# Loading x in larger pieces without a wait, and a new order of all tasks, in a fused attention and gMLP kernel

## Chip, cores and metric

The kernel runs on one core of one Trainium2 chip. The metric is the device time of one execution in microseconds (us), the median of several runs. The core has five engines with a queue each: PE (matrix multiply), DVE (vector), ACT (scalar and activation functions), POOL and SP. Loads and stores are issued by SP, a few by ACT, and are carried out by 16 DMA engines.

## What is computed

Inputs and weights are bf16. x has 2048 tokens of 448 features.

```
h  = x + A(layernorm(x))
h2 = h + B(layernorm(h))

A: qkv = x @ wqkv                       # 16 heads of 28
   each token attends to itself and the 7 tokens 2, 4, ... 14 before it (masked at the start)
   o = softmax(q k^T / sqrt(28)) v;  return o @ wo
B: z = gelu(x @ w_in)                   # 448 -> 2 x 896
   z1, z2 = halves of z;  z2 = layernorm(z2)
   g = w_sp @ z2 + b_sp                 # over the tokens, w_sp is 2048 x 2048
   return (z1 * g) @ w_out
```

## The kernel before

Attention works on nine tiles (`NT`), each of 114 tokens and a halo of 16 before them, in both halves of the sequence at once (s = 0 and 1, 1024 tokens apart), with even and odd tokens on different partitions (w = 0 and 1). A tile of x lies in `xs[:, i, s, :]`. `ln_unit` normalises it: on DVE statistics (`bn1_i_s`, lines 656 and 657) and the normalisation into a ring of four buffers (`nrm1_i_s`, line 674), and in between the reciprocal root (`rs1_i`, two instructions on POOL or ACT). The result is transposed into `xh`: tiles 0 to 2 on PE (`tT1_i`, line 689) with an eviction (`ev1_i`, line 626 or 628), tiles 3 to 8 by a DMA that SP issues (`tD1_i`, line 680) and that stands in SP's queue until the normalisation is done. Matmuls of q and k (`mmq`, `mmk`, line 768) go by groups of tiles: 0; 1; 2 to 4; 5 to 8. They use padded copies of the weights (`cpq`, `cpk`, line 626 on ACT or 628 on DVE); every copy needs all four parts of its weight. Then follow, by tile, v (`mmv`, line 802), scores (`mml`, line 835), exp, the band mask (`mask`, line 857), sums (`mmr`, line 868), the product with v (`mmo`, line 891) and the product with 1/sum (`ot`, line 909).

Then, by blocks of 128 tokens, comes the output projection (`mmy`, line 948) with the residual (`h`, line 956, on x loaded a second time as `x_tm` by the loads `xn0` to `xn3`, line 528), layernorm, a DMA transpose (`tD2`), z2 (`mmz2`, line 968) and z1 (`mmz1`, line 1015), and at the end the product with w_sp (`g`, line 1052, whose result DVE adds the bias to, line 1061) and with w_out (line 1081).

The order is not that of the program text. Every piece of work is a task, numbered as it is created. `SEQ` lists, for SP, POOL, DVE, ACT and PE in this order, the numbers of that engine's tasks in the order of its queue. `Planner.replay` walks through these lists with estimated durations; by them it gives out PSUM banks and ring buffers and emits the instructions. An engine works strictly in its list's order; waits come from the data itself (`Sched.issue`), and a DMA may also wait for tasks in its `waits`. So one late task holds all that stands behind it on its engine.

Before, the x loads of tiles 2 to 8 wait on SP for the q weights:

```
for t in t_xs[i]:
    t.deps += t_w["q"]
    t.waits += t_w["q"]
```

The start of the queues before, with the numbers read as names (`xs2_1` is tile 2, w = 1, both halves of the sequence; `xs0a`, `xs0b` are the halves of tile 0; `wq0` to `wq3` are the parts of the q weight, two of 336 KB and two small ones; `wkv2`, `wkv3` serve k and v; `wo`, `wop` are parts of the output weight):

```
SP   xs1_0 xs0a_1 xs0a_0 xs0b_1 xs0b_0 wq1 wq3 wk0 wop1 wkv3 | xs2_1 xs3_0 xs3_1 xs4_0 xs6_1 xs4_1
     xs2_0 xs7_0 wv0 wv1 xs8_0 xs5_1 wop2 xs8_1 xs6_0 xs5_0 wo1 wop0 tD1_3 xs7_1 tD1_4 wo2 xn1 xn2 ...
ACT  xs1_1 wkv2 wq0 wq2 rs1_1 wk1 rs1_0 ev1_1 cpq1 ev1_0 ...
DVE  bn1_1_0 bn1_1_1 bn1_0_0 nrm1_1_0 nrm1_1_1 bn1_0_1 nrm1_0_0 nrm1_0_1 cpq0 cpk0 cpk1 bn1_3_1 ...
PE   f0 tT1_1 f1 tT1_0 mmq1_0 mmq1_2 mmk1_0 mmk0_0 mmq0_2 mmk1_2 mmq0_0 mmk0_2 mmv0 tT1_2 mml0 mmv1 mmv2 mmk2_1 ...
```

(`f0` and `f1` are 15 and 3 matmuls that only warm PE up; the bar marks where SP waits for the q weights.) The loads of w_sp (`wsp0_b`, `wsp1_b`, line 930) are DMA transposes in two chains of 16, in the order of blocks 0, 8, 1, 9, 2, 10, 3, 11, 4, ...; each waits on SP until the one before it in its chain has landed.

Of the kernel before, what the change touches and what calls it, by code (L numbers as in the profile page):

```python
# [6 lines left out]
D = 448  # L7
DH = 28
FH = 896
# [4 lines left out]
ST = 1024  # L14
# [205 lines left out]
class Planner:  # L220
# [68 lines left out]
    def replay(self, t0=0.7):  # L289
# [13 lines left out]
        for _ in tasks:  # L303
# [34 lines left out]
            if t.nbytes:  # L338
                dma_free = max(dma_free, now + 0.3) + t.nbytes / t.bw / 1000.0
                t.end = dma_free + t.setup  # L340
                self.landed = max(self.landed, t.end)
            else:
                t.end = now + dur + extra
# [11 lines left out]
def bass_sequential_preLN__sliding_local_dilated__mixer_gmlp__prompt_kernel(  # L355
# [18 lines left out]
    with contextlib.ExitStack() as top:  # L374
# [102 lines left out]
        stg_old = r_wl["q"] + [r for i in range(NT) for s in range(2) for r in r_xs[i][s]]  # L477
# [25 lines left out]
        def dve4x(n):  # L503
            return (190.0 + 0.26 * n) / 1000.0

        def dma(eng, name, fn, nbytes, deps=(), reads=(), writes=(), rel=(), store=False, issue=0.5, bw=245.0, after=(), setup=2.0):
            def em():
                rd = list(reads)
                for w in t.waits:
# [645 lines left out]
```

## Time and profile before

| | |
|---|---|
| median of 3 runs | 255.0 us (253.35 to 256.37) |
| the profiled execution, its own time | 255.13 us |
| its span, first to last instruction | 253.4 us |
| PE busy | 237.7 us, 94% of the span |
| DVE, ACT, POOL busy | 138.3, 86.7, 23.4 us |
| mean granted clock of PE | 0.987 |

Busy shares are averages over stages that differ: the first 20 us wait for loads, then attention keeps PE, DVE and ACT busy together, and from about 130 us on PE works almost alone. In a row of the time line, what stands in brackets is how long the engine was idle before it and what ended that. "issue" there means that the profile saw nothing that was waited for.

### The profile page before, as it was taken

What the parts mean: (1) busy time and instruction counts of PE and PEld (TensorE: products, weight loads), DVE (VectorE), ACT (ScalarE), POOL (GpSimd) and SP (SyncE); (2) the same over time, 40 slices, a digit from 0 to 9 for tenths busy, and PEclk for the clock granted to TensorE, in tenths of its full rate; (3) what the DMA queues carried; (4) which work ended last, traced back from release to release, by engine and by line L of the source; (5) the groups of instructions that cost most, each with busy time, mean ns of one, the idle gap of its engine ahead of it and who ended that gap; (6) DMA issues with size and microseconds to landing.
All of it is one profiled execution on the core that took longest, in us unless ns stands there. A gap on an engine that the chain in (4) does not pass through costs nothing.

```text
span 253.4 us, 6573 instructions
## 1 busy us (share of the span) xinstructions
PE 237.7 (94%) x2942; PEld 119.5 (47%) x2952; DVE 138.3 (55%) x278; ACT 86.7 (34%) x110; POOL 23.4 (9%) x61
## 2 busy tenths in 40 slices
PE   7674999987999899999999999999999999999995
PEld 2372665544455454454444444444444444444443
DVE  3585975569599898769881005105700238321573
ACT  2543968676597834857571000000000000000000
POOL 7010200000030203203450000000000000000000
PEclk9997999999799999999999999999999999999999
DMA  5879987568863997695733363310000000010213
GB/s 153 238 189 203 259 97 184 81 106 117 171 169 54 209 221 180 120 131 119 160 84 85 83 153 79 77 26 0 3 0 0 18 0 21 0 36 0 75 36 110
DMA packets 60657, 25.62 MB, mean 101 GB/s; under 512 B 48084, under 2 KB 60484, under 8 KB 60628
## 3 DMA queue, kind: packets, MB, share of 16 engines
q1 hardware_dynamic: 59524, 24.22, 46.1%
q10 hardware_dynamic: 1104, 0.98, 1.4%
q8 instruction: 23, 0.38, 0.6%
q14 instruction: 6, 0.05, 0.1%
HBM read 11.75 MB, written 1.84 MB: 54 GB/s over the span
## 4 chain that ended last, share of the span: by engine, by line
PE 87%; DMA 5%; SPq 4%; issue 3%; DVE 0%
PE psum L1052 38%; PE psum L1081 8%; PE psum L1015 8%; PE psum L768 8%; PE psum L968 7%; PE psum L802 6%; PE psum L948 5%; PE psum L835 3%; SPq L540 3%; PE psum L891 2%; DMA z2p<-in_A_wqkv_dram 2%; DMA xh<-tring 2%; DMA w_in<-in_A_wqkv_dram 1%; PE psum L868 1%; SPq L546 1%
## 5 line engine op out<-in xcount | busy, mean ns | idle before, releaser
L1061 DVE TENSOR_TENSOR ub<-psum,reg 128x512 bf16<-128x512 f32 x28 | 18.8, 687 | 58.5 <-PE psum L1052 40.3
L1052 PE MATMUL psum<-reg,z2p 128*128 128x512 bf16 x219 | 49.2, 379 | 0.3
L1052 PE MATMUL psum<-wspT_lo,z2p 128*128 128x512 bf16 x219 | 48.7, 379 | 0.4 <-issue 0.2
L1052 PEld LDWEIGHTS psum<-wspT_lo,z2p 128*128 128x128 bf16 x224 | 21.8, 98 | 26.5 <-DVE z2p L998 0.4
L1052 PEld LDWEIGHTS psum<-reg,z2p 128*128 128x128 bf16 x224 | 21.8, 98 | 26.5 <-DVE ub L1061 0.4
L768 PE MATMUL psum<-xh,reg 64*128 64x114 bf16 (+3 forms) x448 | 27.2, 271 | 1.1 <-DVE reg L628 1.0
L968 PE MATMUL psum<-w_in,xh 64*128 64x448 bf16 x224 | 22.6, 349 | 0.4 <-DMA xh<-tring 0.4
L1081 PE MATMUL psum<-reg 128*128 128x448 bf16 (+1 forms) x119 | 22.3, 342 | 0.0
L1015 PE MATMUL psum<-xh,w_in 64*128 64x512 bf16 x196 | 22.0, 376 | 0.0
L626 ACT ACTIVATE reg<-psum 128x896 bf16<-128x896 f32 (+4 forms) x24 | 17.8, 758 | 11.0 <-PE psum L802 5.5
L1091 DVE TENSOR_TENSOR tring<-psum,x_tm 128x448 bf16<-128x448 f32 (+1 forms) x17 | 9.8, 594 | 21.1 <-PE psum L1081 21.1
L768 PEld LDWEIGHTS psum<-xh,reg 64*128 64x128 bf16 x448 | 16.3, 93 | 9.9 <-DVE reg L628 1.2
L802 PE MATMUL psum<-w_in,xh 64*128 64x448 bf16 x126 | 15.8, 398 | 4.3 <-issue 4.2
L984 DVE BATCH_NORM_STATS2 st<-z2p 128x6 f32<-128x448 bf16 x32 | 17.5, 611 | 3.2 <-ACT z2p L978 3.2
L850 ACT ACTIVATE reg<-psum 128x928 bf16<-128x928 f32 x18 | 16.4, 943 | 5.4 <-PE psum L835 5.2
L978 ACT ACTIVATE z2p<-psum 128x896 bf16<-128x896 f32 x16 | 13.9, 917 | 9.9 <-PE psum L968 6.5
L1025 ACT ACTIVATE reg<-psum 128x1024 bf16<-128x1024 f32 x14 | 13.9, 1029 | 7.9 <-PE psum L1015 7.9
L1081 PEld LDWEIGHTS psum<-reg 128*128 128x128 bf16 x119 | 11.5, 98 | 10.3 <-DVE tring L1091 0.4
L968 PEld LDWEIGHTS psum<-w_in,xh 64*128 64x128 bf16 x224 | 10.6, 94 | 11.2 <-DMA xh<-tring 0.8
L1015 PEld LDWEIGHTS psum<-xh,w_in 64*128 64x128 bf16 x196 | 9.5, 94 | 11.4
L631 POOL TENSOR_SCALAR rs<-mv 128x2 f32<-128x2 f32 x18 | 5.1, 284 | 105.0 <-DVE mv L657 86.0
L656 DVE BATCH_NORM_STATS2 st<-z2p 128x6 f32<-128x448 bf16 x18 | 11.0, 612 | 6.9 <-DMA z2p<-in_A_x_dram 6.8
(54 smaller groups left out, 202.8 us busy)
## 6 DMA issues: line engine op xcount, KB each, us to landing
w_in<-in_B_w_in_dram SPq DMA_DIRECT2D x4, 672.0 KB, 5.5
x_tm<-in_A_x_dram SPq DMA_DIRECT2D x4, 448.0 KB, 5.2
z2p<-in_A_x_dram SPq DMA_DIRECT2D x15, 112.0 KB, 3.3
out_dram<-tring SPq DMA_DIRECT2D x15, 112.0 KB, 1.8
w_in<-in_A_wqkv_dram SPq DMA_DIRECT2D x3, 336.0 KB, 5.8
reg<-in_A_wo_dram SPq DMA_DIRECT2D x4, 196.0 KB
reg<-in_B_w_out_dram SPq DMA_DIRECT2D x1, 784.0 KB, 5.6
reg<-in_B_b_sp_dram SPq DMA_DIRECT2D x1, 512.0 KB, 4.8
```

The source lines that it names most:

```text
L626: iss("act", lambda e: e.activation(dst, src, AF.Copy), reads=rd, writes=wr)
L768: iss("pe", lambda e, c=c, s=s, gi=gi, lhs=lhs, mov=mov: e.matmul(psum[:, bk[s] * 512 + cw * gi:bk[s] * 512 + cw * gi + cw], lhs, mov, sta ...
L802: iss("pe", lambda e, c=c, s=s: e.matmul(psum[:, bk[s] * 512:bk[s] * 512 + D], xh[64 * s:64 * s + 64, BLK[s][c], 128 * i:128 * i + 128], w ...
L850: iss("act", lambda e: e.activation(E[:, es[0], 2 * n:2 * n + 2, :], pair_view(lb, 0, 8 * JW), AF.Exp, scale=SCALE), reads=[r_bank[lb[0]], ...
L968: iss("pe", lambda e, c=c, s=s: e.matmul(psum[:, zb[s] * 512:zb[s] * 512 + D], xh[64 * s:64 * s + 64, BLK[s][c], 128 * u:128 * u + 128], w ...
L978: iss("act", lambda e: e.activation(z2p[:, u:u + 9:8, D * k:D * k + D], pair_view(zb, 0, D), AF.Gelu_apprx_tanh), reads=[r_bank[zb[0]], r_ ...
L984: iss("dve", lambda e, b=b: e.bn_stats(st3[:, b, k, :], z2p[:, b, D * k:D * k + D]), reads=[r_z2[b][k]], writes=[r_st3[b][k]])
L1015: iss("pe", lambda e, c=c, s=s: e.matmul(psum[:, bk[s] * 512:bk[s] * 512 + 512], w_in[0][64 * s:64 * s + 64, c, 128 * f:128 * f + 128], xh ...
L1025: iss("act", lambda e: e.activation(z1p[f].rearrange("p (s t) -> p s t", s=2)[:, :, 512 * ch:512 * ch + 512], pair_view(bk, 0, 512), AF.Ge ...
L1052: iss("pe", lambda e, b=b: e.matmul(psum[:, gb[0] * 512:gb[0] * 512 + 512], z2p[:, b, 128 * f:128 * f + 128], src[:, b, 512 * (tc % 2):512 ...
L1061: iss("dve", lambda e: e.tensor_tensor(ub[:, us_[0], :], psum[:, gb[0] * 512:gb[0] * 512 + 512], bb[:, 512 * tc:512 * tc + 512], ALU.add), ...
L1081: iss("pe", lambda e, f=f: e.matmul(psum[:, wb[0] * 512 + d0:wb[0] * 512 + d1], z1p[f][:, 128 * m:128 * m + 128], w_out[:, f, d0:d1], star ...
```

## The change

Tiles 3 to 8 of x come in loads of three tiles each, for one half of the sequence and one w (`xs3_10` is tiles 3 to 5, second half, w = 0): eight loads in place of twelve. The wait of x loads for the q weights is dropped. `replay` gets other constants for DMAs (issue 0.62 us and 285 bytes per ns, and 0.4 us ahead of the data), and the dependencies of the statistics are told to it by half of the sequence. All five lists of `SEQ` are new. The constants act only through the lists and the banks and buffers that `replay` hands out; no instruction but the x loads is added or taken away, though some small ones (evictions, copies, the reciprocal roots) move between ACT, DVE and POOL.

```diff
-        for i in range(2, NT):
-            ld_xs(i, 0, "sp")
-            ld_xs(i, 1, "sp")
-            for t in t_xs[i]:
-                t.deps += t_w["q"]
-                t.waits += t_w["q"]
+        ld_xs(2, 0, "sp")
+        ld_xs(2, 1, "sp")
+        for i in (3, 6):
+            for n in range(2):
+                for w in range(2):
+                    ld_xs3(i, n, w, "sp")
...
+        def ld_xs3(i, n, w, eng):
+            lo = ST * n + TQ * i - HALO + w
+            src = X[lo:lo + 2 * TQ + 127, :]
+            src = bass.AP(tensor=src.tensor, offset=src.offset, ap=[[2 * D, 64], [TQ * D, 3], [1, D]])
+            xs_dma("xs%d_%d%d" % (i, n, w), eng, xs[64 * w:64 * w + 64, i:i + 3, n, :], src, 192, [(i + k, n, w) for k in range(3)])
...
-                dma_free = max(dma_free, now + 0.3) + t.nbytes / t.bw / 1000.0
+                dma_free = max(dma_free, now + 0.4) + t.nbytes / t.bw / 1000.0
...
-                tb.append(add("bn%d_%d_%d" % (which, u, n), "dve", 0.76, em, deps=src_deps))
+                tb.append(add("bn%d_%d_%d" % (which, u, n), "dve", 0.77, em, deps=src_deps[n]))
...
-            tt = add("tT%d_%d" % (which, u), "pe", 0.9 if u < 2 else 0.5, em_t, deps=tn + [c_ident], acq=[("ps", 1, bk)],
+            tt = add("tT%d_%d" % (which, u), "pe", 0.55, em_t, deps=tn + [c_ident], acq=[("ps", 1, bk)],
```

The start of the new lists, with names for the numbers:

```
SP   xs1_0 xs0b_1 xs0b_0 xs0a_0 xs0a_1 xs3_10 wk0 wkv3 xs3_11 xs3_00 xs3_01 wq1 wq3 wop2 wop0 wop3 xs2_1 xs2_0 wv1 wv0
     xs6_11 xs6_10 xs6_00 wo0 tD1_3 xs6_01 tD1_4 wo2 xn1 win1_1 wo3 tD1_5 tD1_8 tD1_6 tD1_7 wop1
     wsp0_0 wsp0_8 win1_0 wsp0_1 xn0 wo1 wsp0_9 wsp0_2 xn3 wsp0_10 win1_3 wsp0_3 win1_2 wsp0_11 wsp0_4 xn2 tD2_1 ...
ACT  xs1_1 wkv2 wk1 rs1_1 wq0 rs1_0 wq2 cpk0 ev1_0 evk1_0 evk0_2 cpq0 evq0_2 evk0_0 rs1_2 ...
DVE  bn1_1_1 bn1_0_1 bn1_1_0 bn1_0_0 nrm1_1_0 nrm1_1_1 nrm1_0_0 nrm1_0_1 cpk1 ev1_1 bn1_4_1 bn1_3_1 bn1_4_0 bn1_3_0 cpq1
     nrm1_3_0 bn1_2_0 bn1_2_1 evq1_0 nrm1_3_1 nrm1_2_0 nrm1_2_1 nrm1_4_0 nrm1_4_1 bn1_6_1 bn1_5_0 bn1_5_1 bn1_7_1 bn1_8_1 ...
PE   f0 tT1_1 f1 tT1_0 mmk1_0 mmk0_2 mmk1_2 mmk0_0 mmq0_2 mmq1_0 mmq0_0 mmq1_2 mmv1 tT1_2 mmv0 mmv2 mml0 mmq2_2 mmk2_1 ...
     ... mmk3_3 mmy1 mmo3_0 mmr4 mmo3_1 mmo4_0 mmo4_1 mml5_0 mmv5 ... mmy4 mml8_1 mmr7 mmy5 mmo7 mmr8 mmo8 mmz2_1 ...
```

Later, `tD2_1` comes first of the second transposes instead of `tD2_2`, and the bias load `bb` stands one w_sp load further back than before.

More of the change, by code (lines that the diff above doesn't have):

```diff
@@ L476, in bass_sequential_preLN__sliding_local_dilated__mixer_gmlp__prompt_kernel @@
         kv_old = r_wl["k"] + r_wl["v"]
-        stg_old = r_wl["q"] + [r for i in range(NT) for s in range(2) for r in r_xs[i][s]]
+        stg_old = r_wl["q"] + [r for i in range(NT) for rr in r_xs[i] for r in rr]
         reg2_old = [r for rr in r_q + r_k for r in rr] + [r_qend]
@@ L504, in dve4x, with dma @@
             return (190.0 + 0.26 * n) / 1000.0
-        def dma(eng, name, fn, nbytes, deps=(), reads=(), writes=(), rel=(), store=False, issue=0.5, bw=245.0, after=(), setup=2.0):
+        def dma(eng, name, fn, nbytes, deps=(), reads=(), writes=(), rel=(), store=False, issue=0.62, bw=285.0, after=(), setup=2.0):
             def em():
@@ L532, in ld_x, with xs_dma @@
                 t_x[b] = t
-        t_xs = [[] for _ in range(NT)]
+        t_xs = [[[], []] for _ in range(NT)]
         XT = X.rearrange("(s t) f -> t s f", s=2)
+        def xs_dma(name, eng, dst, src, kb, cover):
+            t = dma(eng, name, lambda e: e.dma_start(dst, src), kb * D * 2, writes=[r_xs[i][n][w] for i, n, w in cover])
+            for i, n, w in cover:
+                t_xs[i][n].append(t)
         def ld_xs(i, w, eng):
@@ L539, in ld_xs @@
             if i:
-                t_xs[i].append(dma(eng, "xs%d_%d" % (i, w), lambda e: e.dma_start(
-                    xs[64 * w:64 * w + 64, i, :, :], XT[lo:lo + 127:2, :, :]), 128 * D * 2,
-                    writes=[r_xs[i][0][w], r_xs[i][1][w]]))
+                xs_dma("xs%d_%d" % (i, w), eng, xs[64 * w:64 * w + 64, i, :, :], XT[lo:lo + 127:2, :, :], 128, [(i, n, w) for n in range(2)])
                 return
-            t_xs[0].append(dma(eng, "xs0a_%d" % w, lambda e: e.dma_start(
-                xs[64 * w + HALO // 2:64 * w + 64, 0, 0, :], X[w:w + 111:2, :]), 56 * D * 2, writes=[r_xs[0][0][w]]))
-            t_xs[0].append(dma(eng, "xs0b_%d" % w, lambda e: e.dma_start(
-                xs[64 * w:64 * w + 64, 0, 1, :], X[ST + lo:ST + lo + 127:2, :]), 64 * D * 2, writes=[r_xs[0][1][w]]))
+            xs_dma("xs0a_%d" % w, eng, xs[64 * w + HALO // 2:64 * w + 64, 0, 0, :], X[w:w + 111:2, :], 56, [(0, 0, w)])
+            xs_dma("xs0b_%d" % w, eng, xs[64 * w:64 * w + 64, 0, 1, :], X[ST + lo:ST + lo + 127:2, :], 64, [(0, 1, w)])
+        def ld_xs3(i, n, w, eng):
[3 more added lines that the diff above has]
+            xs_dma("xs%d_%d%d" % (i, n, w), eng, xs[64 * w:64 * w + 64, i:i + 3, n, :], src, 192, [(i + k, n, w) for k in range(3)])
         t_w = {}
@@ L559, in ld_w @@
             t = dma(eng, "w%s%d" % (p, n), lambda e: e.dma_start(dst, src),
-                    (64 if n > 1 else 384) * len(p) * D * 2, writes=[r_wl[x][n] for x in p], bw=200.0 if n > 1 else 330.0)
+                    (64 if n > 1 else 384) * len(p) * D * 2, writes=[r_wl[x][n] for x in p], bw=285.0)
             for x in p:
@@ L568, in ld_win @@
                 t = dma("sp", "win%d_%d" % (z, n), lambda e, dst=dst, src=src: e.dma_start(dst, src),
-                        (64 if n > 1 else 384) * FH * 2, deps=deps, writes=[r_win[z][n]], bw=200.0 if n > 1 else 330.0, after=after)
+                        (64 if n > 1 else 384) * FH * 2, deps=deps, writes=[r_win[z][n]], bw=285.0, after=after)
                 t_win.setdefault(z, []).append(t)
@@ L704, in bass_sequential_preLN__sliding_local_dilated__mixer_gmlp__prompt_kernel @@
         for i in range(NT):
-            t_xh.append(ln_unit(i, 1, t_xs[i] + ([c_x0] if i == 0 else [])))
+            t_xh.append(ln_unit(i, 1, [t_xs[i][0] + ([c_x0] if i == 0 else []), t_xs[i][1]]))
         fill("f0", 15)
@@ L959, in bass_sequential_preLN__sliding_local_dilated__mixer_gmlp__prompt_kernel @@
             t_h.append(th)
-            t_hT.append(ln_unit(u, 2, [th]))
+            t_hT.append(ln_unit(u, 2, [[th], [th]]))
             tb3 = []
```

58 rows, old and new, of the table SEQ are left out of this document.

## The prediction

> **What bounds the kernel now.** I read the page first, then a table of stages (busy time, granted clock and DMA share in stretches I chose), then the early waits and the time line. The page:
>
> ```profile
> span 253.4 us, 6573 instructions
> PE   7674999987999899999999999999999999999995
> w_in<-in_A_wqkv_dram SPq DMA_DIRECT2D x3, 336.0 KB, 5.8
> x_tm<-in_A_x_dram SPq DMA_DIRECT2D x4, 448.0 KB, 5.2
> ```
>
> TensorE (PE) is nearly full from slice 5 on. Its holes are in the first four slices of 6.3 us; the clock is in the table by stage that follows (columns: stretch, its length, busy us and count of PE, PEld, DVE, ACT, POOL, granted clock, DMA share, GB/s):
>
> ```profile
> 0.00:6.80 6.80, 5.27 (x15) 1.83 (x15) 2.63 (x7) 1.78 (x3) 4.46 (x20) 1.00 0.61 158
> 6.80:9.60 2.80, 1.21 (x10) 0.60 (x10) 2.04 (x7) 1.01 (x3) 0.00 (x0) 1.00 0.90 268
> 12.40:15.60 3.20, 2.34 (x84) 2.22 (x84) 2.56 (x6) 1.20 (x3) 0.23 (x2) 1.00 0.60 147
> 15.60:18.10 2.50, 2.47 (x88) 2.24 (x84) 1.79 (x5) 1.43 (x3) 0.89 (x2) 1.00 0.73 186
> 18.10:22.20 4.10, 0.00 (x0) 0.00 (x0) 3.11 (x10) 2.38 (x7) 0.00 (x0) 1.00 0.89 250
> 22.20:25.80 3.60, 3.54 (x25) 1.78 (x26) 1.78 (x5) 0.78 (x1) 0.19 (x1) 0.53 1.11 191
> ```
>
> From 18.1 to 22.2 PE does nothing, and for the 3.6 us after it runs at 0.53 of its clock. The chain calls the hole "issue", but the loads of the last weights (line 559, issued from 15 to 18 us) say who waits for them:
>
> ```profile
> L559 SPq DMA_DIRECT2D w_in<-in_A_wqkv_dram x2: 489/542/596, 15.6 to 16.3; - x2
>   PE psum L802: 4.2, 1
> DMA to landing us min/median/max: 3.6/4.7/5.9
> ```
>
> The two V loads issue at 15.6 and 16.3; the later one lands at 16.3 + 5.9 = 22.2, where PE starts again. They are late because SP stands still before them:
>
> ```profile
> SPq L176 <- DMA z2p<-in_A_wqkv_dram: 2.4, 1, 2.4
> 6.56 0.47 SPq L559 DMA_DIRECT2D w_in<-in_A_wqkv_dram  x1
> 9.60 5.99 SPq L540 DMA_DIRECT2D z2p<-in_A_x_dram  x8
> ```
>
> SP is idle from 7.0 to 9.6, held by the q weights, then issues eight x loads at about 0.61 us (one takes 1.40) ahead of V. From 12.4 to 18.1 the DMA share is only 0.60 and 0.73: SP's issue sets the rate there, not the memory.
>
> **The change, part by part.** The time line of the front (start, us, engine, line, operation) and the chain after it:
>
> ```profile
> 6.12 0.63 DVE L656 BATCH_NORM_STATS2 st<-z2p 128x6 f32<-128x448 bf16 x1 [0.43 <-DMA z2p<-in_A_x_dram]
> 6.88 0.67 DVE L674 TENSOR_SCALAR tring<-z2p,mv,rs 128x448 bf16<-128x448 bf16 x2
> 7.61 0.56 PE L689 MATMUL psum<-ident,tring 128*128 128x128 bf16 x7 [0.83 <-DVE tring L674]
> 8.01 0.81 PE L620 MATMUL psum<-wspT_lo 128*128 128x512 bf16 x3
> 9.79 1.50 ACT L626 ACTIVATE reg<-z2p 128x1568 bf16<-128x1568 bf16 x1
> 10.42 1.82 PE L768 MATMUL psum<-xh,reg 64*128 64x114 bf16 x56
> 13.26 4.83 PE L768 MATMUL psum<-xh,reg 64*128 64x114 bf16 x168 [1.02 <-DVE reg L628]
> 22.26 2.73 PE psum L802 x14
> 26.47 2.75 PE psum L802 x28
> 29.23 3.10 PE psum L768 x42
> 40.43 1.54 PE psum L768 x14
> ```
>
> *Front of SP.* The first five loads are of the same kinds, so they end near 4.3 as now. Then come xs3_10, wk0, wkv3, three more 168 KB x loads, wq1, wq3, three small wop, two xs2, wv1, wv0. At 0.6 us each (0.4 for a wop) with 0.05 between, wv0 issues at 12.6: 3.7 us earlier, with no wait. With 3.6 to 5.9 us to landing, V is there from 16.2 to 18.5. By bytes: 3.86 MB go before the last V load is done; 1.07 MB have gone by 6.8 (158 GB/s), the rest at 259 (mean of the rows at 268 and 250) takes 10.8 us: 17.6. I take **18**; the upper end, if the DMA can do no more than its 186 GB/s row, is 6.8 + 15.0 = 21.8.
>
> *First matmuls, later.* DVE's list now has bn1_1_1, bn1_0_1, bn1_1_0, bn1_0_0. The second needs tile 0's load, 6.12 by the row above; three statistics at 0.78 end at 8.46, two normalisations at 9.15, so tile 1's transpose moves from 7.61 to 9.2. ACT has wq0's issue (0.55) between the two rstd, so tile 0 is normalised at 10.05; with warm-up matmuls (0.81) the second transpose ends at 11.1. ACT's copy of k (1.50, after wq2's issue at 9.8) ends at 11.3. PE starts k at **11.3 instead of 10.42**. The 224 matmuls take 1.82 + 4.83 = 6.65: 17.95. The copies of q stand behind four statistics of tiles 3 and 4 on DVE (11.2 + 3.1 + 0.62 = 15.0 against 14.6 needed): +0.4. PE now idles 6.8 to 9.2, which may halve its clock for one stretch; between 0 and 2 us, of which I take 0.6. Then q and k end at 19.0 (18.3 to 20.5). V has landed: **V starts at 19.0 instead of 22.26**.
>
> The Trainium skill ("TensorE: Matmul & The Clock Gate", section "HAM oscillation — how this bites in real kernels") asks only for no PE idle gap over about 3.4 us. By it the 2.4 us gap is free and 0.6 us come off the sum; the trace halves the clock after a 1.30 us gap (rows below), so the row decides.
>
> *Half clock.* 14 V matmuls took 2.73 at 22.26 against 1.37 later (28 in 2.75). Without the hole these 1.36 us go.
>
> *To tiles 2 to 4.* Three V groups (4.1), the transpose (0.56) and tile 0's scores (0.63) lead PE to 24.3. The DMA transposes of tiles 3 and 4 bound it: DVE copies q until 15.0, starts tile 3's normalisation when Pool's rstd comes (15.8), takes tile 2's statistics (17.8) and an eviction (0.6), and ends five more normalisations (0.35 each) at 20.2; SP has tD1_3, xs6_01 (0.64) and tD1_4 in line, the last issues at 20.8 and lands in 3.6 (2.9 to 4.4):
>
> ```profile
> L680 SPq DMA_TRANSPOSE xh<-tring x6: 1222/1261/1332, 21.8 to 37.1; - x6
> DMA to landing us min/median/max: 2.9/3.6/4.4
> ```
>
> So PE starts tiles 2 to 4 at 24.6 instead of 29.23: **4.6 us ahead**. xs6_01 now stands behind tD1_3's wait for DVE; it lands near 23.5, and DVE first reads it near 24 (four statistics of other tiles come first), so this costs nothing; if it came 2 us later, DVE would be late by as much for tiles 6 to 8.
>
> *Tiles 5 to 8.* DVE: eight statistics (6.2) from 20.2, six normalisations, mask0 and two evictions: done near 32.0. SP issues the last two transposes at 31.6 and 32.9; the last lands near 36.5. PE gets there at 24.6 + 11.9 = 36.5 (eight groups at 1.05, 3.5 of small work). Now it begins these tiles at 40.43, and has 0.63 of scores still to do that come earlier after: **4.3 ahead** (4.6 less 0.3 for a tight landing).
>
> *Behind that.*
>
> ```profile
> 54.62 0.24 PE L891 MATMUL psum<-reg 64*32 64x58 bf16 x14 [0.95 <-issue]
> 63.18 0.29 PE L835 MATMUL psum<-reg 32*64 32x58 bf16 x12 [1.30 <-issue]
> 63.40 2.79 PE L802 MATMUL psum<-w_in,xh 64*128 64x448 bf16 x14
> 87.07 0.73 PE L891 MATMUL psum<-reg 64*32 64x58 bf16 x68 [0.95 <-issue]
> q8 instruction: 1, 0.02, 3.5%
> 40.40:92.20 51.80, 48.41 (x1368) 25.99 (x1366) 40.03 (x53) 36.60 (x41) 4.49 (x8) 0.97 0.76 143
> 92.20:132.70 40.50, 39.96 (x394) 18.78 (x390) 33.64 (x87) 25.94 (x29) 11.95 (x24) 1.00 0.72 140
> 132.70:253.40 120.70, 117.57 (x557) 55.07 (x565) 38.68 (x76) 1.58 (x2) 0.00 (x0) 1.00 0.17 42
> ```
>
> PE works 48.41 of 51.80 us, DVE 40.03, so a shift passes through. Three stops lie inside a group of equal matmuls, where no data is awaited; a packet of the instruction queue (the q8 row, from 51 to 53 us) precedes the first. So I read them as instruction fetches. The second is followed by half clock (14 matmuls in 2.79). The new order strings small groups together too (mmo3_0, mmr4, mmo3_1, mmo4_0, mmo4_1, mml5_0). All three gone would give 3.2 + 1.4 (2.79 against 1.37) = 4.6; one more with half clock would cost 1.3 + 1.4 = 2.7. I take +0.3, as the new strings are about as many and a little longer. From 92 on PE is the bound and its work is unchanged: 0.
>
> **Sum**, against the profiled execution's 255.13 (span 253.4 and 1.73 around it; the median of the runs is 255.0): −4.3 + 0.3 = −4.0, so 251.1; from the median **251.0**. Alone, with the bounds of landing and clock, 249.6 to 252.4.
>
> **The rivals.** (1) *The stops go as well.* With the second one and its half clock gone (2.7): 251.0 − 2.7 = 248.3. For it: the stops hang on what DMA lies in front of a fetch, and that is all reordered. Against: the strings remain.
>
> (2) *Instruction fetch behind an unbroken stream.* SP no longer pauses, so by 12.4, when wv1 is issued, 3.51 MB are asked for and 1.07 + 5.6 x 0.259 = 2.52 have gone: 1.0 MB, 3.8 us, are in line. If a fetch asked for there queues behind them, PE stops in the q/k groups by about 1.5 (between the 0.95 to 1.30 of the three stops and the 3.8 of the line), and the half clock adds 1.4: 253.9. For it: the three stops. Against: now PE runs through 10.42 to 12.24 and 13.26 to 18.1 without one.
> The Trainium skill ("DMA: Bandwidth & Descriptors", section "Queues, rings and completion order") has each DMA engine go round the queue rows packet by packet, so that a fetch would not queue behind the backlog and the forecast would stay 251.0. The three stops speak against relying on it.
>
> (3) *The loads don't come earlier.* If DMA rather than issue limits 9.6 to 18.1, V lands at 21.8 and the half clock stays: 0.4 gained there, and with tiles 2 to 8 prepared earlier perhaps 1: 254.0. Against: 250 and 268 GB/s in the neighbouring rows.
>
> (4) *Slower: xn2 behind the w_sp chain.* It holds x for h4 to h7 and now stands behind wsp0_4, the ninth of loads that each wait for the one before.
>
> ```profile
> L930 SPq DMA_TRANSPOSE wspT_lo<-in_B_w_sp_dram x8: 1160/1178/1205, 38.9 to 70.9; - x8
> DMA to landing us min/median/max: 3.1/4.4/5.8
> 81.41 1.09 DVE L956 TENSOR_TENSOR x_tm<-psum,x_tm 128x896 bf16<-128x896 f32 x1 [0.18 <-PE psum L948]
> ```
>
> Seven steps took 32.0 us: 4.57 each. The chain would start at 34.7, behind the last transpose (32.9 + 1.3) and a wop (0.5); eight steps, wsp0_4's issue (1.2) and xn2's landing (5.2) give 77.7, and h4 wants it at 81.41 − 4.0 = 77.4: on the edge. If a step takes 5.2 (the longest took 5.8), xn2 lands at 82.7. DVE stands at h4 with mask8, h5 and ot7 queued behind, PE runs dry at mmr8 for 5.3, and the half clock adds 1.4: 257.7. It turns the sign from about 4.85 a step. Against: the bytes of other loads in between are about the same, over eight steps instead of seven, which makes a step shorter.
>
> **How the numbers follow.** Chances: forecast 0.42, (1) 0.17, (2) 0.15, (3) 0.10, (4) 0.16. A measurement here tells about 1% (2.55 us) from no change. Faster by over 1%, below 252.45: forecast and (1), 0.59; within 1%: (2) and (3), 0.25; slower, above 257.55: (4), 0.16. The range leaves out (4)'s end and the lower part of (1): 247.6 to 256.2.
>
> **What would show it.** Right: V's two loads issued before 13.5; first q/k matmul near 11.3; first V matmul from 18 to 20.5 at full clock; tiles 5 to 8 begun near 36; from 132.7 on the same length. Wrong: a hole ahead of V as now; a stop within the q/k groups (2); DVE waiting at line 956 for an x load (4); an idle PE after 130 because line 1061 waits for the bias.

## The result, and the profile after

The changed kernel is **slower**: 258.06 us (median of 20 runs, 254.2 to 262.15) against 253.97 us for the kernel before beside it (20 runs, 251.3 to 258.38). The ratio is 1.0127, with a 95% interval of 1.0083 to 1.0172. The ratio, here and below, goes only by the executions within 1.5% of their kernel's fastest (the medians of all 20 would give 1.016), and the profiled execution of the changed kernel is not among them. The forecast was 251.0, and its range ended at 256.2. The execution that was profiled took 259.99 us, about 1.9 us above the median; its lines are compared with those of before, which took 255.13, so the span differs by 4.9 us and the medians by 4.1, where the ratio stands for 3.2: the lines show the loss somewhat too large.

The page of the changed kernel (span, PE and granted clock in 40 slices, two kinds of load with their time to landing):

```profile
span 258.3 us, 6573 instructions
PE   7369988799699699999999999999999999999995
PEclk9997999899999979999999999999999999999999
z2p<-in_A_x_dram SPq DMA_DIRECT2D x8, 168.0 KB, 5.8
w_in<-in_A_wqkv_dram SPq DMA_DIRECT2D x3, 336.0 KB, 7.4
```

The hole of before around 20 us (its slice 4) is gone and an emptier slice 2 has come; small notches stand in slices 8, 11 and 14, and the 336 KB loads now take 7.4 us to land where they took 5.8. To see where the time went, I cut both executions at about the same places in the work: the start of tiles 2 to 4, of tiles 5 to 8 (40.42 in the old order, whose cut lies 0.7 us behind it), the first z2 block, and the product with w_sp. The cut at 90.4 and 87.7 is the start of the first z2 block in the new order and the place in the old one where as many matmuls are done (1940 and 1955 records); the old order has done a first group of z2, 14 matmuls or 1.5 us, ahead of it. First the changed kernel, then before; columns as in the prediction.

```profile
0.00:27.90 27.90, 19.98 (x371) 13.13 (x372) 18.21 (x49) 13.23 (x21) 7.63 (x31) 0.94 0.94 195
27.90:42.20 14.30, 12.35 (x331) 8.49 (x330) 8.68 (x17) 9.84 (x17) 1.53 (x3) 1.00 1.07 183
42.20:90.40 48.20, 41.48 (x1238) 23.05 (x1239) 35.55 (x46) 34.92 (x39) 3.56 (x6) 0.96 0.65 137
90.40:137.80 47.40, 47.23 (x452) 22.92 (x454) 35.52 (x89) 24.81 (x29) 11.61 (x24) 0.96 0.73 129
137.80:258.30 120.50, 117.37 (x557) 55.23 (x565) 40.66 (x80) 2.76 (x3) 1.30 (x3) 1.00 0.17 40
```

```profile
0.00:29.20 29.20, 20.54 (x371) 12.54 (x373) 17.91 (x49) 14.18 (x25) 6.99 (x29) 0.94 0.80 202
29.20:41.10 11.90, 11.90 (x272) 7.56 (x268) 8.01 (x15) 9.12 (x17) 0.00 (x0) 1.00 0.87 146
41.10:87.70 46.60, 43.21 (x1312) 23.19 (x1307) 35.55 (x47) 34.67 (x40) 3.50 (x6) 0.96 0.72 136
87.70:132.70 45.00, 44.46 (x449) 21.13 (x440) 38.12 (x94) 27.17 (x30) 12.94 (x27) 1.00 0.76 147
132.70:253.40 120.70, 117.57 (x557) 55.07 (x565) 38.68 (x76) 1.58 (x2) 0.00 (x0) 1.00 0.17 42
```

The front gains 1.3 us. The attention behind it loses 4.0 (14.30 + 48.20 against 11.90 + 46.60), the stretch after that 2.4, and the last one is the same. In the attention PE's idle time is 62.50 − 53.83 = 8.67 us where it was 3.39. The time line says in what it lies (between the stops stand four rows that show the clock):

```profile
39.88 0.24 PE L898 MATMUL psum<-reg 64*32 64x58 bf16 x13 [1.95 <-issue]
42.18 4.29 PE L775 MATMUL psum<-xh,reg 64*128 64x456 bf16 x42
49.90 0.42 PE L842 MATMUL psum<-reg 32*64 32x58 bf16 x14 [1.88 <-issue]
50.25 5.54 PE L775 MATMUL psum<-xh,reg 64*128 64x456 bf16 x42
63.41 0.74 PE L955 MATMUL psum<-reg,z2p 64*128 64x448 bf16 x5 [0.21 <-issue]
67.69 0.24 PE L898 MATMUL psum<-reg 64*32 64x58 bf16 x13 [2.25 <-issue]
89.73 0.59 PE L898 MATMUL psum<-reg 64*32 64x58 bf16 x54 [2.30 <-issue]
90.43 4.48 PE L975 MATMUL psum<-w_in,xh 64*128 64x448 bf16 x28
128.81 2.81 PE L975 MATMUL psum<-w_in,xh 64*128 64x448 bf16 x28
```

The five stops sum to 8.59 us of those 8.67; before there were three, 0.95 + 1.30 + 0.95 = 3.20. They are of the same kind, inside groups of equal matmuls where no data is awaited, only about twice as long, apart from the small one at 63.41. After the last of them the clock is halved: 28 matmuls of z2 take 4.48 us where the same 28 take 2.81 later. The rows on both sides of the cut at 90.4 are best taken together, since the group of z2 stands on different sides of it: from tiles 2 to 4 to the product with w_sp the new order takes 109.9 us and the old one 103.5. Of these 6.4 us, 5.4 are stops and 1.7 the half clock at 90.43; all else is 0.7 less. Each order has one more half clock in the attention, worth about 1.3 us in both (42 matmuls in 5.54 instead of 4.29 at 50.25; in the old order at 63.40).

### The profile page after: what moved, and what is told of

Same layout as the page of the kernel before. It is cut to its first block, busy times and chain, and to the rows that moved or that the text cites. A ratio compares the mean times of both kernels' runs of the same rounds, so it can differ in the third digit from the quotient of the medians.

```text
span 258.3 us, 6573 instructions
## 1 busy us (share of the span) xinstructions
PE 238.4 (92%) x2942; PEld 122.8 (48%) x2952; DVE 138.6 (54%) x279; ACT 85.6 (33%) x105; POOL 25.6 (10%) x65
## 4 chain that ended last, share of the span: by engine, by line
PE 88%; issue 4%; DMA 2%; SPq 2%; DVE 2%; POOL 1%; DVEq 0%; POOLq 0%
PE psum L1059 37%; PE psum L775 10%; PE psum L975 9%; PE psum L1088 8%; PE psum L1022 8%; PE psum L955 5%; PE psum L809 5%; PE psum L842 3%; DMA w_in<-in_A_wqkv_dram 2%; PE psum L898 2%; SPq L538 1%; PE psum L875 1%; DVE st L663 1%; POOL rs L639 1%; DVE reg L635 0%
## 5 line engine op out<-in xcount | busy, mean ns | idle before, releaser
L1059 PEld LDWEIGHTS psum<-wspT_lo,z2p 128*128 128x128 bf16 x224 | 21.8, 98 | 26.6 <-issue 0.4
L775 PE MATMUL psum<-xh,reg 64*128 64x114 bf16 (+3 forms) x448 | 29.5, 291 | 3.6 <-DVE reg L635 2.0
L775 PEld LDWEIGHTS psum<-xh,reg 64*128 64x128 bf16 x448 | 19.1, 103 | 12.4 <-issue 2.2
L975 PE MATMUL psum<-w_in,xh 64*128 64x448 bf16 x224 | 23.6, 367 | 0.1
L1088 PE MATMUL psum<-reg 128*128 128x448 bf16 (+1 forms) x119 | 21.7, 341 | 0.0
L991 DVE BATCH_NORM_STATS2 st<-z2p 128x6 f32<-128x448 bf16 x32 | 17.8, 609 | 6.4 <-ACT z2p L985 6.4
L975 PEld LDWEIGHTS psum<-w_in,xh 64*128 64x128 bf16 x224 | 11.5, 98 | 11.4 <-issue 2.6
L639 POOL TENSOR_TENSOR rs<-rs,nhalf 128x2 f32<-128x2 f32 x20 | 15.3, 766 | 1.7
L635 DVE CAST reg<-psum 128x912 bf16<-128x912 f32 (+3 forms) x10 | 9.8, 984 | 8.2 <-PE psum L775 7.7
```

What stands on the lines that cost most here:

```text
L639: iss("pool", lambda e: e.tensor_tensor(dst, dst, nh, ALU.pow), reads=rr + [r_nhalf], writes=rr)
L775: iss("pe", lambda e, c=c, s=s, gi=gi, lhs=lhs, mov=mov: e.matmul(psum[:, bk[s] * 512 + cw * gi:bk[s] * 512 + cw * gi + cw], lhs, mov, sta ...
L975: iss("pe", lambda e, c=c, s=s: e.matmul(psum[:, zb[s] * 512:zb[s] * 512 + D], xh[64 * s:64 * s + 64, BLK[s][c], 128 * u:128 * u + 128], w ...
L991: iss("dve", lambda e, b=b: e.bn_stats(st3[:, b, k, :], z2p[:, b, D * k:D * k + D]), reads=[r_z2[b][k]], writes=[r_st3[b][k]])
L1059: iss("pe", lambda e, b=b: e.matmul(psum[:, gb[0] * 512:gb[0] * 512 + 512], z2p[:, b, 128 * f:128 * f + 128], src[:, b, 512 * (tc % 2):512 ...
L1088: iss("pe", lambda e, f=f: e.matmul(psum[:, wb[0] * 512 + d0:wb[0] * 512 + d1], z1p[f][:, 128 * m:128 * m + 128], w_out[:, f, d0:d1], star ...
```

## Experiments

In the expectations, where letters stand for theories, S says that the stops inside groups set the time behind 27 us, and F that the front (loads and first matmuls) sets it. All times are medians, and each ratio is to the kernel before, run beside it, and worked out as above.

### Which part of the order costs the time

Two hybrids cut the task lists where the plan stands at 22.5 us (about the scores of tile 0). One has the new front and, behind it, the old order:

```diff
 SEQ, code of the changed kernel
   tasks that the new plan starts before 22.5 us: in the new order
-  all others: in the new order
+  all others: in the order of before
```

> The kernel after with its own lists up to the scores of tile 0 and the transposes of tiles 3 and 4, and the order of before behind that. Theory F and S: the front as after, tiles 2 to 4 begin near 28 (1.3 ahead of before); behind that the stops are those of before in size, about 1 us each; time 0 to 1% below before. Rival (the front is what loses): 1% above before, like the kernel after.

Measured: 255.39 us, ratio 1.0063 (1.0026 to 1.0099), where 0 to 1% below before was expected. In its profile tiles 2 to 4 begin only at 30.93 (27.89 in the changed kernel, 29.06 before), behind a stop of 2.77 us at 23.04; behind that its two longest stops are 0.76 and 0.54 us. The other has the old front, loads and wait, and the new order behind:

```diff
 SEQ, code of the kernel before
   tasks that the old plan starts before 22.5 us: in the order of before
-  all others: in the order of before
+  all others: in the new order
```

> The reverse: small loads, wait and front order of before, and the order of after behind the scores of tile 0. Theory F and S: front as before with the hole of 4 us ahead of V; behind that four stops of about 2 us as in after; time 1.5 to 3% above before. Rival (the front is what loses): within 0.5% of before.

Measured: 258.82 us, ratio 1.0207 (1.0157 to 1.0257). The time line of this second one:

```profile
28.38 5.34 PE L744 MATMUL psum<-xh,reg 64*128 64x342 bf16 x70 [3.00 <-DMA xh<-tring]
41.59 0.29 PE L867 MATMUL psum<-reg 64*32 64x58 bf16 x12 [3.12 <-issue]
68.22 0.29 PE L867 MATMUL psum<-reg 64*32 64x58 bf16 x13 [2.82 <-issue]
92.64 0.59 PE L867 MATMUL psum<-reg 64*32 64x58 bf16 x53 [2.02 <-issue]
```

So the loss comes with the order behind the front, without the new loads, and its three long stops (four of about 2 us were expected) stand at the same matmuls as in the changed kernel (12 or 13, 13, and 53 or 54 left of a group). The new front alone gains nothing; with the old order behind it, it costs 0.6%.

### What the stops are

I numbered PE's matmuls and weight loads in order of time, and set beside them the packets of the instruction queue, which the page of the changed kernel counts:

```profile
PE 238.4 (92%) x2942; PEld 122.8 (48%) x2952; DVE 138.6 (54%) x279; ACT 85.6 (33%) x105; POOL 25.6 (10%) x65
q8 instruction: 23, 0.38, 0.6%
```

5894 instructions and 23 packets make 256 to a packet. In the 14 profiles of this study there are 61 stops of over 0.6 us (from one start to the next) around these block ends, all at number 420 to 455 plus 256 k; 56 of them end 2.2 to 2.95 us after the start of packet k. In the last stage of the two kernels a packet starts when PE is at number 112 to 120 of its block (but for the one at the stage's start); in the attention it starts later than that, and by how much is the "wait" of this table (read from the trace: us from number 115 to the packet's start; us that PE needs from 115 to the block's end; the gap at that end, from start to start):

```
             block  wait  needs  gap          block  wait  needs  gap
after           3   4.42   4.58  2.14  before     6   2.59   4.22  1.14
after           5   5.33   5.63  2.07  before     8   3.69   4.82  1.49
after           8   4.91   4.89  2.45  before    13   5.15   6.39  1.15
after          13   4.52   4.84  2.48
```

A gap is the wait, plus 2.3 to 2.8 us from the packet's start to the next instruction, less what PE needs. By this table the new order's gaps are longer because its packets wait longer (4.4 to 5.3 us against 2.6 to 5.2); PE's need is about the same (4.6 to 5.6 against 4.2 to 6.4). If these gaps are what costs the time, moving the block ends must move the stops and change the time, with no other work touched. The pad is 30 small warming matmuls, 60 instructions, put into a hole of PE at 6.4 us, where it waits for x anyway:

```diff
+for _ in range(30 if name == "f0" else 0):
+    iss("pe", lambda e: e.matmul(psum[:, fb[0] * 512:fb[0] * 512 + 64], warm[:, 0:128], warm[:, 0:64]),
+        reads=[r_warm], writes=[r_bank[fb[0]]])
```

> The kernel after with 30 small matmuls more among the warm-up ones, where PE is idle anyway (6.8 to 9.5 us): 60 more instructions on PE ahead of everything. Theory S (PE stops where a block of 256 instructions ends): every stop comes 30 matmuls (60 instructions) earlier in the order: the stop inside the mmo0 group after 51 matmuls goes to 21, the one inside mml3 after 50 to 20, and each is as long as fetch and strings then make it (0 to 3 us). Rival (the stops wait for data or banks of a certain task): they stay at the same matmuls. Time within 1.5% of after either way.

Measured: 254.92 us, ratio 0.9973 (0.9917 to 1.0029); the changed kernel without the pad has 1.0127. Some of its stops, and the first z2 block:

```profile
57.35 0.21 PE L845 MATMUL psum<-reg 32*64 32x58 bf16 x3 [1.44 <-issue]
62.57 0.50 PE L901 MATMUL psum<-reg 64*32 64x58 bf16 x43 [1.01 <-issue]
85.58 0.24 PE L901 MATMUL psum<-reg 64*32 64x58 bf16 x12 [1.26 <-issue]
86.67 4.51 PE L978 MATMUL psum<-w_in,xh 64*128 64x448 bf16 x28
```

The stop that stood with 13 matmuls left of its group now stands with 43 left: 30 matmuls earlier, exactly the pad. It is 1.01 us long instead of 2.25, and the one at the end 1.26 instead of 2.30. The stops of 1.95 and 1.88 us are gone, and others of 0.6 to 1.4 us have come. The front is as before (tiles 2 to 4 begin at 27.84, against 27.89), and z2 begins at 86.67 instead of 90.43: of these 3.8 us, 2.4 are stops (those over 0.6 us sum to 6.0, against 8.4) and 1.25 is the half clock of 50.25, which does not come. So 60 instructions that compute nothing are worth 1.5% of the time.

Can the price of a place be worked out? I took the waits as one flat 3.4 us and the 2.55 us behind the packet (the flat rule, or place theory), and looked for pads that make the sum of gaps large or small. Here the 15 warming matmuls are cut into more, smaller ones, so that their columns stay nearly the same:

```diff
-for _ in range(n):
+for k in range(105 if name == "f0" else n):
+    m = 64 if name == "f0" and k < 103 else 512
     iss("pe", lambda e, m=m: e.matmul(psum[:, fb[0] * 512:fb[0] * 512 + m], warm[:, 0:128], warm[:, 0:m]),
```

This is the changed kernel with 180 instructions more; the next two are the kernel before with 184 (2 and 105 matmuls) and with 148 (4 and 85).

> The changed kernel; its first 15 warming matmuls of 512 columns become 2 of 512 and 103 of 64, nearly the same columns and 180 more instructions of TensorE (matmuls and weight loads), so that every end of 256 instructions falls 90 matmuls earlier in the work. Place theory: a stop is as long as the packet's wait (put flat at 3.4 us) plus 2.55 us to the first instruction, less the time that TensorE needs from instruction 115 of the block to its end; with the stretches of the changed kernel's profile that gives 6.3 us of stops for the kernel as it is and 15.5 us for this one, so some 9 us more: 264 to 267, ratio to before 1.04 to 1.05. Wait theory: the stretches hardly matter, since the packet's own wait (1.3 to 6 us from packet to packet in the profiles) decides; the sum is drawn anew, 3 to 9 us instead of 8.5: 252 to 259, ratio 0.99 to 1.02. If neither holds and the stops hang on the tasks, 258 and stops in the same groups as in the changed kernel.

Measured: 263.49 us, ratio 1.0367 (1.03 to 1.0433). The stops, with the starts of tiles 2 to 4 and of z2:

```profile
25.62 1.12 PE L810 MATMUL psum<-w_in,xh 64*128 64x448 bf16 x10 [1.73 <-issue]
30.62 5.34 PE L776 MATMUL psum<-xh,reg 64*128 64x342 bf16 x70
53.46 1.94 PE L776 MATMUL psum<-xh,reg 64*128 64x456 bf16 x18 [1.41 <-issue]
68.38 0.25 PE L843 MATMUL psum<-reg 32*64 32x58 bf16 x7 [3.22 <-issue]
93.22 0.30 PE L899 MATMUL psum<-reg 64*32 64x58 bf16 x16 [2.94 <-issue]
93.62 4.30 PE L976 MATMUL psum<-w_in,xh 64*128 64x448 bf16 x28
```

> The kernel before with the same edit, 2 matmuls of 512 columns and 105 of 64, so 184 more instructions of TensorE. Place theory: the sum of stops goes from 7.9 us (by the same flat 3.4 us; measured 3.3) to 10.9, 3 us more: 257, ratio 1.012. Wait theory: drawn anew, 3 to 9 us where there are 3.3 now: 253 to 259, ratio 0.995 to 1.02, with stops in other groups. Stops by tasks: 254 and the stops of before at 54.6, 63 and near 90.

Measured: 253.53 us, ratio 0.9998 (0.9962 to 1.0035).

> The kernel before with 4 matmuls of 512 columns and 85 of 64, 148 more instructions of TensorE. Place theory: this is the best place of the ends for these lists, 6.3 us by the flat rule where 0 gives 7.9: 252.3, ratio 0.993. Wait theory: drawn anew, 3 to 9 us: 253 to 259, and no better than the kernel with 184. Stops by tasks: 254.

Measured: 253.64 us, ratio 0.9993 (0.9955 to 1.0031). In the new order the time came close to what the place theory said (263.5, against 264 to 267), but by luck. The rule wanted some 9 us more of stops. From tiles 2 to 4 to z2 this profile takes 63.0 us (30.62 to 93.62) where the changed kernel takes 62.5, and its stops there sum to 8.2 us, against 8.4. Most of what it loses stands in the front, 2.7 of the 4.0 us between the two spans: the k weights landed later, PE began k at 14.17 instead of 12.72, and a block's end stops V for 1.73 us.

In the old order the flat rule misses both times: it said 3 us more and 1.7 less, and nothing changed. It also gives the unpadded kernels the wrong sign: 7.9 us of stops before and 6.3 after, where 3.2 and 8.4 are measured. What it lacks is the wait, which differs from packet to packet (1.0 to 9.0 us in the attention of these profiles). So the block's end says where PE stops, and moving the ends by 30 matmuls is worth 1.5%; how long a stop is, and with it the loss of the new order, cannot be had from the place alone.

What makes a packet wait? One suspect is the line of the DMA engines. In the next kernel all loads of w_sp and the bias go behind the last transpose of the second layernorm, so that the attention's later part has a quiet DMA; the loads are late for their use, and the kernel's end waits for them:

```diff
-chain([t_wsp[b][0] for b in S_ORDER], t_xh[NT - 1])
+chain([t_wsp[b][0] for b in S_ORDER], t_hT[NU - 2])
 SP: all wsp0, wsp1 and bb moved behind the last tD2
```

> The kernel after with all w_sp loads moved behind the last transpose of the second layernorm, so that from about 50 to 75 us hardly a DMA is in flight; the other weight loads crowd together at 38 to 50. Its time is far above (w_sp is late for the last stage, 15 us or more) and is not the question. Theory S (a stop is an instruction fetch that stands in the DMA line): fetches between 52 and 75 us start within 1 us of their place in the program instead of 3 to 5, and the stop of 2.25 us (near 67) is below 0.6; stops in the crowded part stay at 1.5 to 3. Rival (the stops come from the new order itself: PE simply runs through a block faster than one can be fetched): the stop near 67 stays above 1.5.

Measured: 315.38 us, as the end must be. The stretch from 52 to 75 us, and its first and last stop:

```profile
52.00:75.00 23.00, 20.30 (x478) 10.16 (x480) 11.65 (x13) 14.37 (x16) 0.93 (x2) 0.80 0.02 5
52.99 0.42 PE L818 MATMUL psum<-reg 32*64 32x58 bf16 x14 [2.98 <-issue]
71.16 0.24 PE L874 MATMUL psum<-reg 64*32 64x58 bf16 x13 [1.71 <-issue]
```

With DMA at 5 GB/s the same stop (13 left) is still 1.71 us, against 2.25 with DMA at 137 (the changed kernel's row from 42.2 on); the packet's wait is 4.24 us against 4.91. The expectation of a stop below 0.6 us fell, and the rival's, above 1.5, holds. Between these two executions the line of loads is some 0.5 us of that stop; the first one, whose packet started at 50.23, ahead of the quiet stretch, even grew (2.98 against 1.88). What else holds a packet back was not found.

### Why the front gained so little

The wait for the q weights alone, dropped from the kernel before:

```diff
-                t.waits += t_w["q"]
```

> The kernel before with one line taken out: x loads of tiles 2 to 8 no longer wait for the q weights. Lists, sizes and constants stay. Theory F (all DMAs, whichever queue issues them, are served in the order of issue, so loads asked for early stand in front of the weights that are needed first): SP issues 2.5 us earlier, V lands at 19.5 to 21 instead of 22.2, the hole of 4.2 us ahead of V shrinks by 1 to 2.5, time 0.3 to 1% less. Rival (issue by SP was the limit, as the prediction had it): V lands by 19, the hole and the half clock after it go, 4 us or 1.6% less. Rival (the wait kept the line short for the weights): V no earlier, 0 to 1% more.

Measured: 252.05 us, ratio 0.994 (0.9905 to 0.9975). V lands at 19.95 and its first matmul stands at 20.34, as theory F has it. This one line gains 0.6%, and the whole change loses 1.3%. The loads of three tiles, without the wait, in the old lists:

```diff
 code of the changed kernel
-SEQ: new lists
+SEQ: lists of before; each load of three tiles stands where the first of its three single loads stood
```

> The kernel after with the lists of before (the x loads of three tiles stand where the first of their small loads stood): loads of three tiles, no wait, old order of everything else. Theory F and S (S: the loss behind 30 us comes from the new order on PE, which puts strings of small matmuls where instruction fetches wait behind DMAs): the front within 1 us of before, three stops of about 1 us as before, time within 1% of before. Rival (the large loads themselves cost): the front 2 us or more late and time 1% or more above before.

Measured: 255.33 us, ratio 0.9985 (0.9938 to 1.0031). Here ten x loads stand ahead of V, eight of 168 KB and two of 112 KB (1568 KB), where the kernel before has eight of 112 KB (896 KB). V lands at 24.58, and PE waits for it:

```profile
24.67 2.80 PE L785 MATMUL psum<-w_in,xh 64*128 64x448 bf16 x14 [4.08 <-issue]
```

So what stands in front of V counts; loads and bytes both grew here, so the two are not told apart. V was expected within 1 us of before and is 2.4 us late. The time is still that of before, since from tiles 2 to 4 to the product with w_sp this kernel takes 101.1 us instead of 103.7, with no half clock in it. The changed kernel with the q weights ahead of the x loads:

```diff
-SP  ... wk0 wkv3                 ; ACT ... wk1 rs1_1 wq0 rs1_0 wq2
+SP  ... wk0 wkv3 wq1 wq3 xs3_10  ; ACT ... wk1 wq0 wq2 rs1_1 rs1_0
```

> The kernel after with the four q loads issued ahead of the x loads of tiles 3 to 5: on SP xs0a_1, wk0, wkv3, wq1, wq3, xs3_10 and on; on ACT wq0 and wq2 right behind wk1. Theory F (one line in order of issue): q lands 2 to 4 us earlier (12.5 to 14 instead of 17.1), the hole of 2 us between k and q goes; V does not land earlier (21 to 22), so the hole moves in front of V; tiles 2 to 4 begin within 1 us of after; time 0 to 0.6% below after, that is 0.7 to 1.3% above before. Rival (the queue of ACT has its own share of the DMA engines, and q was late for another reason): q lands near 17 as before.

Measured: 259.22 us, ratio 1.019 (1.0116 to 1.0264): above the 0.7 to 1.3% that were expected, though by its interval not told apart from the changed kernel. The q weights landed by 12.64 us instead of 17.1, but V still at 21.39, and in the hole's place came the end of PE's first instruction block:

```profile
22.20 1.04 PE L751 MATMUL psum<-xh,reg 64*128 64x114 bf16 x34 [2.02 <-issue]
```

The same stop stands in the hybrid with the new front (2.77 us at 23.04). This profile took 259.23 us, the median, and has the changed kernel's four stops at the same matmuls, 0.99, 1.29, 2.26 and 2.25 us long. The last of this row has before's lists without the wait, and two x loads and an output weight moved behind V:

```diff
-SP  ... xs6_1 ... xs7_0 wv0 wv1 ... wop1 earlier
+SP  ... wv0 wv1 xs6_1 xs7_0 wop1 ...
-                t.waits += t_w["q"]
```

> The kernel before without the wait, and on SP the x loads of tiles 6 and 7 (two of 112 KB) and one small load of wo (28 KB) moved behind the V weights. Theory F: 252 KB less stand in front of V, which lands about 1 us earlier than with the wait alone (18.5 to 19.5 instead of 20.0); the transposes of tiles 3 and 4 then bound tiles 2 to 4, which begin 0 to 0.8 us earlier; time 0.6 to 1% below before. Rival (the line's order matters little): same as without the wait alone, 0.6% below.

Measured: 252.1 us, ratio 0.993 (0.9884 to 0.9976). V's two loads landed at 17.28 and 19.88, the later one no earlier than without the move (19.95), and the first block's end stops PE for 1.55 us at 19.47. The expected 1 us did not come, so the bytes issued in front of V do not give its landing by themselves.

### A version faster than both

The last kernel is that one with 140 instructions more of PE (5 warming matmuls of 512 columns and 80 of 64), the place with the smallest sum by the flat rule.

> The kernel before without the wait for weights, with two x loads and one output weight behind the V weights (ratio 0.993 by itself, stops 5.4 us), and 5 matmuls of 512 columns and 80 of 64, 140 more instructions of TensorE. Place theory: 9.0 us by the flat rule goes to 6.5: 249.7, ratio 0.983. Wait theory: drawn anew, 3 to 9 us around its 5.4: 250 to 256, ratio 0.985 to 1.005. Stops by tasks: 252.1.

Measured: 251.66 us, ratio 0.9887 (0.9837 to 0.9937). It beats both kernels. From its own base (0.9884 to 0.9976) it is not told apart, so what the pad adds here is open, and the 249.7 us of the place theory did not come. In its profile the clock is granted in full from 5.2 to 251.0 us.

## Why the prediction was wrong

The signs in the profile that the prediction named can be read off one by one. The front of the changed kernel:

```profile
11.65 1.13 SPq L566 DMA_DIRECT2D w_in<-in_A_wqkv_dram x2
9.47 0.56 PE L696 MATMUL psum<-ident,tring 128*128 128x128 bf16 x7 [2.80 <-DVE tring L681]
12.72 3.25 PE L775 MATMUL psum<-xh,reg 64*128 64x114 bf16 x112 [1.65 <-ACT reg L633]
17.93 4.71 PE L775 MATMUL psum<-xh,reg 64*128 64x114 bf16 x112 [1.96 <-DVE reg L635]
22.48 1.48 PE L809 MATMUL psum<-w_in,xh 64*128 64x448 bf16 x14
27.89 4.31 PE L775 MATMUL psum<-xh,reg 64*128 64x342 bf16 x56
```

**Front of SP: the issue was right, the landing wrong.** V's loads issue at 11.65 and 12.29, "before 13.5" as forecast (12.6). They land at 19.03 and 21.40, not at 18; before, the later one landed at 22.17. So V is issued some 4 us earlier and lands 0.8 us earlier. The step that failed here is the rate of 259 GB/s up to the landing. The bytes do move at such rates:

```profile
6.80:9.60 2.80, 0.13 (x3) 0.14 (x4) 2.68 (x9) 1.00 (x4) 0.00 (x0) 1.00 1.07 262
9.60:12.40 2.80, 1.47 (x17) 0.94 (x15) 1.74 (x5) 1.24 (x1) 0.00 (x0) 1.00 1.11 247
12.40:15.60 3.20, 2.88 (x106) 2.80 (x108) 2.75 (x8) 2.23 (x4) 0.86 (x2) 1.00 1.13 232
15.60:18.10 2.50, 0.54 (x21) 0.37 (x16) 0.85 (x3) 0.88 (x1) 1.75 (x7) 1.00 1.14 278
18.10:22.20 4.10, 4.10 (x102) 3.97 (x98) 3.34 (x11) 2.06 (x5) 0.00 (x0) 0.58 0.90 162
```

By 18.1, 3.90 MB have moved (153 GB/s up to 6.8, then the first four rows), more than the 3.86 that the forecast counts up to V, so loads issued later have part of them. The first of the 16 parts of the last V load ends at 17.77, about when the forecast has it, the 15th at 19.91 and the last at 21.40; a load is there when its slowest part is. (Before, the 15th and last ended at 20.73 and 22.17.) By the prediction's own count, 3.86 MB less 153 GB/s times 6.8 us (1.04 MB) in 14.6 us are 193 GB/s. The bound of 186 GB/s, 21.8 us, was the right end to take. Rival 3 (the DMA is the limit, not the issue) has the landing right; its half clock came elsewhere. But V's landing did not set V's start: PE was at q and k until 22.5.

**First matmuls and q weights.** PE's k starts at 12.72, not 11.3, since the k weights land at 10.67 and 10.98 behind x loads. The q copies start at 17.23, where the forecast has them done at 15.0: the weights' last parts land at 16.11 and 17.08. The prediction timed these copies by DVE's list alone and did not ask when their weights land under the load it had just worked out for V. Their rows name POOL as releaser, which had long been done; it is the loads:

```profile
17.23 1.51 ACT L633 ACTIVATE reg<-z2p 128x1568 bf16<-128x1568 bf16 x1 [2.10 <-POOL ones L719]
17.25 0.62 DVE L635 COPY reg<-z2p 128x1568 bf16<-128x1568 bf16 x1 [1.96 <-POOL ones L719]
```

How the loads of SP and ACT landed (us, read from the trace):

```
       wkv3   xs3_11  wq1    wq3    wq0 (ACT)  wq2 (ACT)  wop0   wop3   wv1    wv0
issued 5.23   5.75    7.74   8.39   8.42       9.20       9.45   9.79   11.65  12.29
landed 10.98  11.50   13.76  15.59  16.11      17.08      16.55  17.28  19.03  21.40
```

They land nearly in the order of issue, whichever engine issued them. The Trainium skill ("DMA: Bandwidth & Descriptors", section "Queues, rings and completion order") gives SP and ACT a ring each on the same 16 engines, served in turn by packets; from that one would expect wq2, 56 KB with only wq0 ahead of it on ACT's ring, to pass SP's backlog. In this trace it does not: issued at 9.20, it lands between wop0 and wop3, which SP issues at 9.45 and 9.79. The order is not strict: in the kernel with 180 instructions more a load that ACT issued at 8.53 lands at 15.69, ahead of one that SP issued at 7.38 (17.32).

**Half clock.** V's 14 matmuls take 1.48 us as forecast (2.73 before). But behind the gaps of 1.65 and 1.96 us it comes earlier: from 18.1 to 22.2 the clock is 0.58, and 112 q and k matmuls take 4.71 instead of 3.25. The gain of 1.36 was given back. Against the forecast of 19.0, V starts at 22.48, later than before (22.26): k began 1.4 late, the gap ahead of the last q and k matmuls is 1.96 where the forecast had 0.4, and the half clock cost about 1.3 (3.25 + 4.71 less 6.65) where it had 0.6.

**Tiles 2 to 8.** They start at 27.89 and 42.18 where the forecast had 24.6 and 36.1, and before 29.06 and 40.42. The first gain is 1.2 us, not 4.6, and it comes from V's full clock. By 42.18 the first stop has already taken more than that.

**Behind that: the term that decides.** The step that failed is the term of +0.3 for the stops, with the reason that the new strings are "about as many and a little longer". In the profile the stretch from tiles 2 to 4 to the product with w_sp measured +6.4, of which the stops are +5.4 and the half clock behind the last of them +1.7. The mechanism, instruction fetches that stop PE, was right; the size was not. The trace of before already held the 256, and with it the places where PE could stop under the new lists. It did not hold the length: PE's need up to the four ends (4.6 to 5.6 us) is about that of before, the packets waited longer, and why they did stays open.

The Trainium skill ("Runtime: NRT & Kernel Launch", section "Instruction fetch mechanics") has blocks of 256 instructions fetched while the one before executes, at a cost that is "mostly hidden". The 256 agree with these traces. Hidden they are in the last stage, with its long matmuls; in the attention they cost 8.4 us of 258.

**From 92 on: 0.** The last stage agrees (120.5 and 120.7), but the half clock at 90.43 was not counted.

**The other rivals.** (1) The stops did not go: their sum rose from 3.2 to 8.4 us. (2) A fetch behind the unbroken stream of loads stops PE in the q and k groups: not in the changed kernel, where q's weights are so late that the packet is there in time, but in three of its variants (2.02, 2.77 and 2.16 us). (4) fell: xn2 issues at 70.75 and lands at 74.44, and DVE's adds at line 963 wait only for PE, 4.6 us in all. The sign came from a case that the prediction had only as "one more stop with half clock, 2.7", under its own forecast and without a chance of its own: it came to 6.4, with 1.3 instead of 4.3 gained in front of it.

**Half clock and gaps.** The prediction weighed the rule of the Trainium skill ("TensorE: Matmul & The Clock Gate", section "HAM oscillation — how this bites in real kernels"), a gap over about 3.4 us, against a stop of 1.30 us that was followed by half clock. Neither holds as a threshold: in the changed kernel the clock halves after 1.96, 1.88 and 2.30 us and does not after 1.95 and 2.25, all under 3.4. The clock records of the 14 profiles show more: within an execution all changes of the clock lie whole multiples of 3.41 us apart, and in the first 100 us it went from full to half only behind a step of 3.41 us in which PE was busy for 2.11 us or less (though not behind every such step). The gap of 2.25 us lies across two steps, with PE busy 2.12 and 2.25 us in them; that of 1.88 leaves 1.97 in one.

## What to carry to other kernels

Where PE works through strings of small matmuls, lay the ends of each 256 matmuls and weight loads over the order before you believe a gain of one per cent. They say where PE may stop, not for how long; a pad of a few dozen tiny instructions in an idle place moves them, and its profile says how much of a difference is only that. A load issued earlier behind the same bytes lands hardly earlier: cost it to its slowest part, and do the same for every other load in that line, since here it was the q weights and not V that held PE. Try the one line that is not an order (here the wait) by itself first: it gained 0.6% where the whole change lost 1.3%.

## What the runs showed of the hardware

- PE's stops lie at fixed numbers of its instruction stream, every 256, whatever the work: 61 stops in 14 profiles, and 56 of them end 2.2 to 2.95 us after an instruction packet starts. The wait of these packets, 1.0 to 9.0 us in the attention, was mostly not the DMA backlog where that was taken away (4.24 us with DMA at 5 GB/s, 4.91 with it); its cause stays open.
- Under a backlog a load's first and last of 16 parts are 3.6 us apart (17.77 and 21.40), the last alone 1.5 us behind the one before it, and loads of two issuing engines land nearly in order of issue.
- The granted clock changes in steps of 3.41 us: all changes within an execution lie on one grid, so that a gap of 1.88 us, most of it inside one step, was followed by half clock and one of 2.25 us across two was not.
